# K first, weight words in one row, and the state's update joined to P U: a DeltaNet and SwiGLU kernel on one core

## The chip, the core and the metric

The kernel runs on one core of a Trainium2 chip. The core has a matrix engine (TensorE, PE in the profile, whose weight loads are shown apart as PEld), a vector engine (VectorE, DVE), an activation engine (ScalarE, ACT), a general engine (GpSimd, POOL) and an engine that only issues transfers (SyncE, SP). Each runs its own list of instructions in order, and waits at an instruction until the semaphores that it names have been counted up. The metric is the time of one execution on the device in microseconds (us); the median of several executions is given.

## The reference

The first stage is a delta rule with a state of 48 x 48 for each of 4 x 8 heads, over 768 steps. The second is a feed-forward layer on the 3072 rows of 384 that come out of it.

```python
k_n = k / (np.linalg.norm(k, axis=-1, keepdims=True) + 1e-06)
for t in range(S):
    y[:, :, t] = q_t @ state
    v_old = state @ k_t
    state = state + beta_t * outer(k_t, v_t - v_old)
# x = y, its heads side by side: (3072, 384)
xn = x / sqrt(mean(x * x) + 1e-06) * rms_g
out = (silu(xn @ w_gate) * (xn @ w_val)) @ w_out
```

The weights (384 x 1536 twice, and 1536 x 384) are 64-bit numbers: the kernel takes each apart into its 32-bit words and makes a 32-bit number of them. Everything is computed in 32-bit numbers.

## The kernel before

**Chunks.** The 768 steps are cut into 12 chunks of 64. For a chunk, `norms` makes the norms of K, `prep` the triangular system of the chunk and its inverse, `qpart` the matrix P of the products of Q and K, and `recur` uses them. `prep` transposes K (helper `turn`, L509), multiplies K by itself (`scores`, L532), writes the products to DRAM (dkk) and reads them back in another layout (at), scales them by beta (L646), and makes the inverse in 15 steps of a product and a sum on VectorE (L693, L699). The result (x or acc, L716, L720) goes through DRAM again (dx) into mt, m1bd and x2bd; two merges (L775, L799) fill its last block. `recur` multiplies the state by K and by Q (L840), forms r (L854), multiplies by the inverse to get u (`mr`, L886), and adds P U to the output (`pu`, L900). It normalises the rows (L940 to L990) and transposes them into xf (L986), and it adds K U to the state (`ku`, L1019, then L1028).

**Feed-forward.** Chunks 0 and 1 go through `ffn_plain`: L1064 multiplies by w_gate and w_val, L1071 takes Silu, L1072 forms hf, L1046 multiplies by w_out. From chunk 2 on, `ffn` forms two chunks' halves with 15 products in place of 18 (L1157, gathered by L1167 and L1169), and `down` multiplies by w_out with 7 in place of 8 (L1214). The factors for these are made once, by `factors` (L1122).

**Weights.** `weights` brings 18 pieces of 128 x 768 numbers into three buffers (`raw`), in SP's queue. For each, L460 on ScalarE scales the high words, L448 and L451 on VectorE shift and mask bits of it, L456 forms the other part from the low words, and the two are added: on TensorE, with a copy after it, for the first three pieces (L472, L473, L477), on VectorE for the rest (L480).

**Order.** The program is not issued in the order of the code. `Plan.add` records each operation with an engine, an assumed duration, a priority and the keys that it reads and writes. `Plan.run` builds an order in 60 rounds, each with slightly altered priorities (`SHAKE`, and the generator's seed), and keeps the one whose assumed end is earliest. A transfer's `after` is the time in this plan before which it isn't placed; on the chip it is no wait, and only the transfer's place in its queue comes of it. `op.port` makes the plan keep such operations of VectorE and GpSimd apart in time. PSUM's eight banks are handed out in the plan as groups come free. Until 70 us of the plan, gaps on TensorE are filled with multiplications of the identity by itself into a spare bank (`fillers`, L1312), which nobody reads.

Of the kernel before, what the change touches and what calls it, by code (L numbers as in the profile page):

```python
# [11 lines left out]
FP32 = mybir.dt.float32  # L12
U32 = mybir.dt.uint32
# [14 lines left out]
STICK = 1.0  # L28
SHAKE = 0.25

# [21 lines left out]
def fillers(a, b):  # L52

    n, t = 0, max(a, 2.0)
    while t < b - 0.3:
        n, t = n + 1, t + (0.43 if t < 6.5 else 0.26)
    return n


class Plan:  # L60
# [150 lines left out]
    def run(self, free, filler=None, until=0.0):  # L211
        self.first_priorities()
        best = None
        self.ends = []
        rng = random.Random(19)
        for k in range(ROUNDS):
# [30 lines left out]
def kernel(  # L247
# [96 lines left out]
    raw = [more[:, 1536 * i : 1536 * i + 1536].bitcast(I64) for i in range(NRAW)]  # L344
    cvb = [tflat[:, 512:1280], more[:, 4608:5376]]
    o_sb = [tmp[:, 3 + p, 0:DM] for p in range(2)]
    extra = [more[:, 3072 * h : 3072 * h + 3072].rearrange("p (x m n) -> p x m n", x=2, m=6) for h in range(2)]
    exkeys = [[("raw", 0), ("raw", 1)], [("raw", 2), ("o", 1)]]

# [70 lines left out]
    def weights():  # L420
# [14 lines left out]
        for n, (dst, src, keys) in enumerate(todo):  # L435
            pr = (30 if n < 9 else CV2) + 0.2 * n
            i, a = n % NRAW, n % NCV
            parts = dst.shape[1]
            rdst = raw[i].rearrange("p (a c) -> p a c", a=parts)
            dma(rdst, src, (0.1 if n == 0 else 3 + 2 * n), w=[("raw", i)], dur=0.7, work=3.06, after=(0.8, 5.0, 16.7, 24.5, 24.5, 33.3, 50.0)[n] if n < 7 else 53.0)  # L440
            words = raw[i].bitcast(U32).rearrange("p (a n two) -> p a n two", a=parts, two=2)
            low, high = words[:, :, :, 0], words[:, :, :, 1]
            u = dst.bitcast(U32)
            cc = cvb[a].rearrange("p (a n) -> p a n", a=parts)
            cvk = [("o", 1)] if a else [("tmp", 1), ("tmp", 2)]

            def s2(u=u):
                nc.vector.tensor_scalar(out=u, in0=u, scalar1=3, scalar2=None, op0=ALU.logical_shift_left)  # L448

            def s4(u=u, cc=cc):  # L450
                nc.vector.tensor_scalar(  # L451
                    out=cc.bitcast(U32), in0=u, scalar1=0xFF800000, scalar2=None, op0=ALU.bitwise_and
                )

            def s5(low=low, cc=cc, by=2.0**-52):
                nc.vector.scalar_tensor_tensor(out=cc, in0=low, scalar=by, in1=cc, op0=ALU.mult, op1=ALU.mult)  # L456

            P.add("ACT", 0.84, lambda high=high, dst=dst: nc.scalar.activation(out=dst, in_=high.bitcast(FP32), func=ACTF.Prelu, scale=2.0**-112, alpha=2.0**32), pr, r=[("raw", i)], w=[("cvw", n)])  # L460
            P.add("DVE", 0.66, s2, pr, w=[("cvw", n)])
            P.add("DVE", 0.66, s4, pr, r=[("cvw", n)], w=cvk)
            P.add("DVE", 1.0, s5, pr, r=[("raw", i)], w=cvk)
            done = []
            if n < NPE:
                for x_ in range(2):
                    ps = Group()
                    cut = slice(2 * x_, 2 + x_)
                    m = 512 - 256 * x_

                    def s6(ps=ps, dst=dst[:, cut], cc=cc[:, cut], m=m):
                        nc.tensor.matmul(ps.t[:, 0:m], ident, dst, start=True, stop=False)  # L472
                        nc.tensor.matmul(ps.t[:, 0:m], ident, cc, start=False, stop=True)  # L473

                    P.add("PE", 0.0035 * m, s6, pr, r=cvk + [("cvw", n), "ident"], w=[("cvp", n, x_)], ps=ps, size=8)
                    done.append(("cv", n, x_))
                    P.add("ACT", A(m), lambda dst=dst[:, cut], ps=ps, m=m: nc.scalar.copy(dst, ps.t[:, 0:m].rearrange("p (a n) -> p a n", n=256)), pr, r=[("cvp", n, x_), ("cvw", n)], w=[done[-1]], last=ps)  # L477
            else:
                done.append(("cv", n))
                P.add("DVE", 0.97, lambda dst=dst, cc=cc: nc.vector.tensor_tensor(out=dst, in0=dst, in1=cc, op=ALU.add), pr, r=cvk, w=[("cvw", n), done[-1]])  # L480
            for key in keys:
                ready.setdefault(key, []).extend(done)
# [4 lines left out]
    def load(c, what):  # L487
        t0 = c * C
        pk, pq, pv = ((-5, 1, 12), (5, 29, 36))[c] if c < 2 else (due(c, 150), due(c, 99), due(c, 70))
        for key, t, src, pr in (("k2", k2[c % NK], k, pk), ("q2", q2, q, pq)):  # L490
            for g in range(2):
# [3 lines left out]
                s = src.rearrange("b (y g) t e -> g t (b y) e", g=2)[g, t0 : t0 + C]  # L495
                dma(dst, s, pr, w=[(key, c % NK if key == "k2" else 0, g)], dur=0.7, work=1.02, eng="ACT" if c == 0 and g and key == "k2" else "SP", after=((0.8, 0.0, 0.0), (7.8, 20.8, 0.0))[c]["kqv".index(key[0])] if c < 2 else 60.3)
        if "v" in what:
            for bb in range(2):
                s = v[2 * bb : 2 * bb + 2, :, t0 : t0 + C, :].rearrange("p h t e -> t (p h) e")
                dma(vt[64 * bb : 64 * bb + 64], s, pv, w=[("v", bb)], dur=0.85, work=1.02, after=(30.4, 34.6)[c] if c < 2 else 60.0)  # L500

# [75 lines left out]
    def prep(c):  # L577
# [61 lines left out]
        for par in range(2):  # L639
            dma(at_[64 * par : 64 * par + 64].rearrange("p j t -> p (j t)"),  # L640
                dk.rearrange("i g x j t -> (i g x) (j t)"), pd, r=dkeys, w=[("at", par)], dur=0.56, work=1.8, eng="SP" if par or c else "ACT")
        bt = beta_b[:, c]
# [175 lines left out]
    def recur(c):  # L818
# [93 lines left out]
        for h in halves:  # L912
# [4 lines left out]
            for bb in range(2):  # L917
# [6 lines left out]
                else:  # L924
                    P.add("DVE", V(192 * len(h)), lambda dst=dst, f=src: nc.vector.tensor_copy(out=dst, in_=f()), pr, r=[gu[bb]], w=w, last=gu[bb])
        for h in halves:
            gy = groups(psy, h)
            P.rows = 64
            P.add("PE", 0.49 * len(h), lambda h=h: pu(h), py, r=ptk + uk(h), w=gy, ps=gy, size=64 * len(h))
            P.rows = 128  # L930
# [62 lines left out]
        if c > 1:  # L993
            X = lambda a, n, step=1: xf[:, a : a + step * (n - 1) + 1 : step]
            for dst, a, b_, op, n in (
# [10 lines left out]
                    out=dst, in0=a, in1=b_, op=op  # L1006
                ), pxv, r=[("xp", 0)], w=["xc", ("xp", 1)])
        if c < NCH - 1:
            pss = [Group(), Group()]

            def ku():
                for b in range(B):
                    for j in range(2):
                        for d in range(2):
                            for g in range(2):
                                rows = slice(64 * g, 64 * g + 64)
                                x_ = 4 * b + 2 * j + d
                                n = 48 * (2 * b + j)
                                nc.tensor.matmul(pss[g].t[64 * d : 64 * d + D, n : n + D], kn[rows, x_, 0:D], u_[rows, x_])  # L1019

            P.rows = 64
            P.add("PE", 0.98, ku, py + 2, r=kkeys_(c) + [("k2p", c % NK)] + uk((0, 1)), w=pss, ps=pss, size=128)
            P.rows = 128
# [237 lines left out]

    setup()
    load(0, "kqv")
    load_small()
# [81 lines left out]
```

## Time and profile before

| | |
|---|---|
| median of 3 executions | 717.38 us (717.36 to 718.38) |
| the profiled execution | 717.67 us |
| its span, first to last instruction | 716.0 us |
| TensorE busy | 701.5 us (98%) |
| VectorE busy | 553.6 us (77%) |
| ScalarE busy | 314.0 us (44%) |
| GpSimd busy | 152.7 us (21%) |
| transfers | 54.68 MB |
| mean granted clock of TensorE | 0.993 |

Times in the profile count from the start of the span. A busy TensorE is not one at its peak: the ends of matmuls are modelled, so that a short wait inside a run of them can be hidden in the busy time. The starts of weight loads (PEld) show it better. PEclk is the clock that TensorE was granted, in tenths of the full one, over 40 slices of 17.9 us. "<-" in square brackets names what ended an idle time. The queues SPq and ACTq show when transfers were issued, not when they landed.

### The profile page before, as it was taken

The numbers are of one execution on the slowest core, as the hardware profiler recorded it, in microseconds if no ns is written. First come the engines' busy times: TensorE is split into PE (matmuls) and PEld (weight loads), VectorE is DVE, ScalarE is ACT, GpSimd is POOL, SyncE is SP. The second block draws the span as 40 slices with busy tenths as digits, with TensorE's granted clock in tenths as the row PEclk, the third lists the DMA queues.
The fourth block names the chain that finished last, engine by engine and source line by source line (L and its number), as shares of the span: only waits on it lengthen the run. The fifth ranks groups of instructions, "written<-read, shape, count | busy, mean of one in ns | idle before, by whom it ended". The sixth has DMA issues, their size and how long they took to land.

```text
span 716.0 us, 23540 instructions
## 1 busy us (share of the span) xinstructions
PE 701.5 (98%) x10178; PEld 652.9 (91%) x10178; DVE 553.6 (77%) x1128; ACT 314.0 (44%) x732; POOL 152.7 (21%) x150
## 2 busy tenths in 40 slices
PE   8998999999999999999999999999999999999997
PEld 7797877777799999998999999999999999999997
DVE  4898999998967958947967967975968958847473
ACT  5613654232345436354345255355355354344331
POOL 4200307004315132204213303203213231000000
PEclk9997999999999999999999999999999999999999
DMA  8756798141154251242234153153162071030000
GB/s 171 210 124 165 157 261 219 23 66 43 35 90 77 39 111 28 47 72 60 57 59 83 37 96 61 34 88 64 38 109 47 12 118 27 15 63 2 23 1 23
DMA packets 210071, 54.68 MB, mean 76 GB/s; under 512 B 199216, under 2 KB 202288, under 8 KB 209968
## 3 DMA queue, kind: packets, MB, share of 16 engines
q1 hardware_dynamic: 205120, 52.26, 36.3%
q8 instruction: 80, 1.31, 0.8%
q10 hardware_dynamic: 4848, 0.92, 0.7%
q14 instruction: 23, 0.19, 0.1%
HBM read 40.83 MB, written 12.32 MB: 74 GB/s over the span
## 4 chain that ended last, share of the span: by engine, by line
PE 80%; DVE 15%; DMA 2%; issue 2%; SPq 1%; ACT 0%; DVEq 0%
PE bank L1157 38%; PE bank L1214 18%; PE bank L1064 6%; PE bank L1046 3%; PE bank L840 3%; PE bank L532 2%; DVE acc L699 2%; PE bank L509 2%; PE bank L799 2%; PE bank L886 2%; DVE acc L693 1%; DMA beta_b<-in_beta_dram 1%; PE bank L900 1%; DVE w_in L480 1%; PE bank L775 1%
## 5 line engine op out<-in xcount | busy, mean ns | idle before, releaser
L1167 DVE TENSOR_TENSOR tmp<-tmp,bank 128x512 f32<-128x512 f32 x180 | 122.0, 685 | 85.4 <-PE bank L1157 74.5
L1157 PE MATMUL bank<-xf,w_in 128*128 128x128 f32 x1440 | 181.5, 277 | 0.0
L1157 PEld LDWEIGHTS bank<-xf,w_in 128*128 128x128 f32 x1440 | 169.8, 192 | 2.3 <-issue 0.4
L1157 PE MATMUL bank<-xf,more 128*128 128x128 f32 x960 | 124.8, 277 | 0.0
L1157 PEld LDWEIGHTS bank<-xf,more 128*128 128x128 f32 x960 | 115.6, 192 | 1.7 <-DVE tmp L1167 0.4
L1169 ACT COPY tmp<-bank 128x512 f32<-128x512 f32 x120 | 68.6, 584 | 82.4 <-PE bank L1157 58.2
L699 DVE TENSOR_REDUCE acc<-acc 128x30 f32<-128x90 f32 (+4 forms) x180 | 85.1, 473 | 6.2
L1173 ACT ACTIVATE tmp<-tmp 128x256 f32<-128x256 f32 x120 | 49.7, 416 | 88.5 <-DVE tmp L1167 88.1
L693 DVE TENSOR_TENSOR acc<-acc,at 128x60 f32<-128x60 f32 (+4 forms) x180 | 63.5, 353 | 8.7 <-POOL at L676 5.9
L1214 PE MATMUL bank<-wo_sb,hf 128*128 128x192 f32 x360 | 63.8, 328 | 0.0
L1174 DVE TENSOR_TENSOR hf<-tmp 128x256 f32<-128x256 f32 x120 | 51.9, 445 | 12.9 <-ACT tmp L1173 11.6
L1214 PEld LDWEIGHTS bank<-wo_sb,hf 128*128 128x128 f32 x360 | 58.2, 190 | 0.3
L646 POOL TENSOR_TENSOR at<-at,beta_b 128x1024 f32<-128x1024 f32 x10 | 25.7, 2574 | 145.2 <-DMA at<-dkk 122.4
L1312 PE MATMUL bank<-ident 128*128 128x128 f32 x298 | 42.0, 304 | 1.4 <-POOL ident masks.py:199 1.4
L554 POOL TENSOR_TENSOR knrm<-ksum,half 128x16 f32<-128x16 f32 x12 | 35.9, 2992 | 33.8 <-DVE ksum L553 33.8
L720 POOL COPY acc<-acc 128x128 f32<-128x128 f32 x40 | 17.1, 458 | 116.4 <-DVE acc L699 115.6
L1312 PEld LDWEIGHTS bank<-ident 128*128 128x128 f32 x298 | 39.5, 215 | 2.5 <-POOL ident masks.py:199 1.4
L1046 PE MATMUL bank<-wo_sb,hf 128*128 128x384 f32 x96 | 34.3, 491 | 0.3 <-DVE r L854 0.3
L1064 PE MATMUL bank<-xf,w_in 128*128 128x256 f32 x144 | 33.6, 382 | 0.0
L1064 PE MATMUL bank<-xp,w_in 128*128 128x256 f32 x144 | 33.4, 383 | 0.0
L1064 PEld LDWEIGHTS bank<-xf,w_in 128*128 128x128 f32 x144 | 26.8, 190 | 4.9
L1064 PEld LDWEIGHTS bank<-xp,w_in 128*128 128x128 f32 x144 | 26.7, 190 | 4.4 <-issue 0.2
(164 smaller groups left out, 1045.9 us busy)
## 6 DMA issues: line engine op xcount, KB each, us to landing
at<-dkk SPq DMA_DIRECT2D x23, 256.0 KB, 3.9
q<-in_q_dram SPq DMA_DIRECT2D x24, 192.0 KB, 3.7
more<-in_moe_w_gate_dram SPq DMA_DIRECT2D x6, 768.0 KB, 6.1
more<-in_moe_w_val_dram SPq DMA_DIRECT2D x6, 768.0 KB, 6.3
more<-in_moe_w_out_dram SPq DMA_DIRECT2D x6, 768.0 KB, 7.5
vt<-in_v_dram SPq DMA_DIRECT2D x24, 192.0 KB, 4.1
out_dram<-tmp SPq DMA_DIRECT2D x48, 96.0 KB, 2.2
k<-in_k_dram SPq DMA_DIRECT2D x23, 192.0 KB, 3.8
```

Source lines behind the costliest of these rows:

```text
L554: P.add("POOL", 2.95, lambda: nc.gpsimd.tensor_tensor(out=knrm[i2], in0=ksum[i2], in1=half, op=ALU.pow), pn, r=[("ksum", i2), "half"], w=[ ...
L693: nc.vector.tensor_tensor(out=acc[:, 1:3, 0:n, j + 2 : W].rearrange("p a i t -> p i a t"), in0=acc[:, old, 0:n, j : j + 2, None].to_broadc ...
L699: nc.vector.tensor_reduce(out=acc[:, new, 0:n, j + 2 : W], in_=acc[:, lo : lo + 3, 0:n, j + 2 : W].rearrange("p a i t -> p i t a"), axis=A ...
L1046: nc.tensor.matmul(po[p].t[:, 0:DM], hf[:, spot(f), 128 * p : 128 * p + 128], wo_sb[:, spot(f)], start=(f == f0), stop=(f == f1 - 1), skip ...
L1064: nc.tensor.matmul(ps.t[:, TOK * side : TOK * side + TOK], w_in[:, side, h_, 3 * t + i_, n : n + 128], x_[:, 2 * t : 2 * t + 2].rearrange( ...
L1157: nc.tensor.matmul(g.t[:, 128 * z : 128 * z + 128], fac[:, side, 128 * f : 128 * f + 128], xf[:, xs], start=(begin and z == 0), stop=False ...
L1167: P.add("DVE", V(512), lambda t=t, g=g: nc.vector.tensor_tensor(out=t, in0=t, in1=g.t, op=ALU.add), -1, r=[g], w=[tk], last=g)
L1169: P.add("ACT", A(512), lambda t=t, g=g: nc.scalar.copy(t, g.t), -1, r=[g], w=[tk], last=g)
L1173: P.add("ACT", A(256), lambda t=t: nc.scalar.activation(out=t[:, 0:256], in_=t[:, 0:256], func=ACTF.Silu), -1, w=[tk])
L1174: P.add("DVE", V(256), lambda t=t, f0=f0, p=p: nc.vector.tensor_tensor(out=hf[:, spot(f0) : spot(f0) + 2, 128 * p : 128 * p + 128], in0=t[ ...
L1214: nc.tensor.matmul(g.t[:, 0:192], a_[:, f], b_[:, f], start=(begin and f == 0), stop=(f == 5), skip_group_check=True)
L1312: nc.tensor.matmul(warm[:, 0:128], ident, ident)
```

## The change

Line numbers below are those of the kernel before; those of the changed kernel lie 3 to 30 lines further on.

- The first transfer on SP is now half of K, where it was Q; Q follows. The other half of K is on ScalarE's queue in both.
- The fillers ahead of the first work are 13, whatever the plan says; elsewhere a filler counts 0.24 us, where it was 0.43 or 0.26.
- The scaled high words of a weight go to a row of 768 numbers that lie together (`cva`, two copies, one in unused columns of xf, one at the end of more), where they went to the weight's final place. L448 shifts them there, L451 masks them from there, and only the last addition writes to the final place.
- For chunks 2 to 10 `ku` is issued within the operation of `pu`, with four banks taken together. For chunks 0 and 1 it stays apart.
- The `after` of the early transfers of K, Q, V, at and the weights are changed.
- The operations of `setup` no longer count for `op.port`.
- Seed 77 where it was 19, `SHAKE` 0.12 where it was 0.25, and the assumed durations of L448, L451, L456 (0.57, 0.57, 0.96) and of `ku` (0.76).

```diff
-SHAKE = 0.25
+SHAKE = 0.12
...
-    n, t = 0, max(a, 2.0)
+    if a == 0.0:
+        return 13
+    n, t = 0, a
     while t < b - 0.3:
-        n, t = n + 1, t + (0.43 if t < 6.5 else 0.26)
+        n, t = n + 1, t + 0.24
...
-        rng = random.Random(19)
+        rng = random.Random(77)
...
+    cva = [xf[:, 6:12].rearrange("p a n -> p (a n)"), more[:, 5376:6144]]
...
-after=(0.8, 5.0, 16.7, 24.5, 24.5, 33.3, 50.0)[n] if n < 7 else 53.0)
+after=(7.5, 5.0, 19.2, 27.2, 18.7, 33.3, 47.0)[n] if n < 7 else 48.8)
...
-            u = dst.bitcast(U32)
+            top, cc = cva[a], cvb[a]
+            u = top.bitcast(U32)
...
-            P.add("ACT", 0.84, lambda high=high, dst=dst: nc.scalar.activation(out=dst, in_=high.bitcast(FP32), func=ACTF.Prelu, scale=2.0**-112, alpha=2.0**32), pr, r=[("raw", i)], w=[("cvw", n)])
+            P.add("ACT", 0.84, lambda high=high, top=top: nc.scalar.activation(out=top, in_=high.bitcast(FP32), func=ACTF.Prelu, scale=2.0**-112, alpha=2.0**32), pr, r=[("raw", i)], w=cak)
...
-                        nc.tensor.matmul(ps.t[:, 0:m], ident, dst, start=True, stop=False)
+                        nc.tensor.matmul(ps.t[:, 0:m], ident, top, start=True, stop=False)
...
-                P.add("DVE", 0.97, lambda dst=dst, cc=cc: nc.vector.tensor_tensor(out=dst, in0=dst, in1=cc, op=ALU.add), pr, r=cvk, w=[("cvw", n), done[-1]])
+                P.add("DVE", 0.97, lambda dst=dst, top=tiled(top), cc=tiled(cc): nc.vector.tensor_tensor(out=dst, in0=top, in1=cc, op=ALU.add), pr, r=cvk + cak, w=[done[-1]])
...
-after=((0.8, 0.0, 0.0), (7.8, 20.8, 0.0))[c]["kqv".index(key[0])] if c < 2 else 60.3)
+after=((0.0, 1.4, 0.0), (8.6, 25.0, 0.0))[c]["kqv".index(key[0])] if c < 2 else 56.8)
...
-after=(30.4, 34.6)[c] if c < 2 else 60.0)
+after=(30.4, 40.0)[c] if c < 2 else 60.0)
...
-eng="SP" if par or c else "ACT")
+eng="SP" if par or c else "ACT", after=41.2 if c == 1 else 0.0)
...
+            if 1 < c < NCH - 1:
+
+                def both_u(h=h):
+                    pu(h)
+                    ku()
+
+                P.add("PE", 1.74, both_u, py, r=ptk + uk(h) + kkeys_(c) + [("k2p", c % NK)], w=gy + pss, ps=gy + pss, size=256)
+                P.rows = 128
+                continue
...
     setup()
+    for op in P.ops:
+        op.port = False
     load(0, "kqv")
```

## The prediction

> **What bounds the kernel now.** I read the page first, then the chain of waits, then the timeline of the first 130 us, since most of the edits are there.
>
> ```profile
> PE 701.5 (98%) x10178; PEld 652.9 (91%) x10178; DVE 553.6 (77%) x1128; ACT 314.0 (44%) x732; POOL 152.7 (21%) x150
> ...
> PEclk9997999999999999999999999999999999999999
> ```
>
> TensorE is the bound, and its clock is full but for one dip near 55 us. In the chain, in order of time (start us, length, what):
>
> ```profile
> 333.98 1.09 PE bank L1157 x8
> 335.06 1.08 PE bank L900 x64
> ...
> 342.30 0.89 PE bank L1157 x8
> ...
> 379.23 2.01 PE bank L840 x128
> ```
>
> These pieces give prices. Eight 128-column passes are 0.89, or 0.111 each; the same eight cost 1.09 where a block of small matmuls follows, so entering such a block costs 0.20. One block is 1.08, two in a row 2.01 and not 2.16, so leaving costs 0.15. Reading the other pieces in the same way, a pass is 0.112 (L1157), 0.1625 (L1214), 0.216 (L1064), 0.3225 (L1046), 0.109 (transposes); a small block is 0.93 (L840, L886, L900, L532, L751), 0.71 (L1019), 0.85 (L799), 0.43 (L775). The order of the program from the first L1064 (75.04 us) on holds 2400, 840, 288, 96 and 226 passes, 97 small blocks (22 of L840, 20 of L532, 11 each of L886, L900, L775 and L799, 10 of L1019, one of L751) worth 81.7 us, and 76 entries with 76 exits: 268.8 + 136.5 + 62.2 + 31.0 + 24.6 + 81.7 + 76 x 0.35 = 631.4 us. The last load ends at 711.3, 636.3 after the first. So only 4.9 us of that stretch are stalls, of which 2.5 lie at 124 us:
>
> ```profile
> 117.38 3.01 DVE L480 TENSOR_TENSOR w_in<-w_in,tmp 128x768 f32<-128x768 f32 x1
> ...
> 126.35 0.66 PE L509 MATMUL bank<-ident,k 128*128 128x128 f32 x4 [1.67 <-DVE hf L1072]
> ```
>
> There VectorE, 97% busy from 72 to 120 us, is late with hf because a sum of 0.96 took 3.01 beside GpSimd's scaling of at. The time is thus: start of the stream + 631.4 + stalls + a tail of 4.7 (to 716.0). What sets the start is the first 75 us:
>
> ```profile
> 7.83 0.84 ACT L550 ACTIVATE r<-k 128x768 f32<-128x768 f32 x1 [3.92 <-DMA k<-in_k_dram]
> ...
> 18.37 0.84 SPq L363 DMA_DIRECT2D dkk<-pt  x2
> ...
> 20.84 0.49 SPq L363 DMA_DIRECT2D at<-dkk  x1
> ...
> 24.64 0.91 ACT L460 ACTIVATE w_in<-more 128x768 f32<-128x768 f32 x1 [0.93 <-DMA more<-in_moe_w_gate_dram]
> ...
> 28.18 1.22 DVE L646 TENSOR_TENSOR at<-at,bk 128x1024 f32<-128x1024 f32 x1
> ```
>
> K lands at 7.83 because its half on SP is issued third, at 2.57; dkk leaves SP at 18.37 though pt is ready at 16.15, behind beta loads; L646 starts at 28.18 because a weight that came at 24.6 is converted ahead of it on VectorE. Later:
>
> ```profile
> 53.97 1.31 PE L751 MATMUL bank<-ident,mt 32*32 32x32 f32 x64 [1.54 <-DMA mt<-dx]
> 55.21 2.08 PE L1312 MATMUL bank<-ident 128*128 128x128 f32 x8
> 59.05 1.08 PE L775 MATMUL bank<-m1bd,kk 128*32 128x64 f32 x32 [1.77 <-DVE m1bd L764]
> 60.06 1.23 PE L1312 MATMUL bank<-ident 128*128 128x128 f32 x4
> 61.22 1.92 PE L799 MATMUL bank<-x2bd,yn 128*32 128x128 f32 x16
> 63.07 2.24 PE L1312 MATMUL bank<-ident 128*128 128x128 f32 x10
> ```
>
> The array runs at half clock here: L751 takes 1.11 and L799 1.07 for chunk 1 at full clock. And L775 waits for VectorE's m1bd, which stands in its order behind 13.3 us of conversions and steps (44.8 to 58.07).
>
> [...]0.213 per filler pass to 13 us, 0.111 after. [...]L451 reads 3x256 and writes 768 for w_in, and 768 to 768 for wo_sb:
>
> ```profile
> L451 DVE TENSOR_SCALAR more<-w_in x6: 944/949/953, 19.6 to 142.5; 128x768 uint32<-128x768 uint32 x6
> L451 DVE TENSOR_SCALAR more<-wo_sb x3: 559/560/560, 76.7 to 146.4; 128x768 uint32<-128x768 uint32 x3
> ```
>
> [...]
>
> **The change part by part.** *K first.* With its half at 0.79, K lands near 5.0 (the ACT half took 3.7 from 0.79). The 13 fillers hold TensorE to 1.41 + 26 x 0.2125 = 6.9, so transposes start 0.9 earlier, not 2.8. Then L519 at 7.9, L551 8.6, GpSimd's power 9.8 to 12.75 (2.92), pt 13.25 to 14.55: 1.6 ahead of 16.15. On SP, dkk is now moved ahead of the last two beta loads, so it leaves at 14.6 and 15.1; at is issued near 17.5 (before: 20.84), behind a weight issued at 16.2. By 5.4 from issue, as before, that weight lands at 21.6. VectorE from 14.55: L621 0.95, one conversion 2.15, sums and bk 1.4 to 19.1, second norm (power 2.9) to 22.2, pt 1.3, the other conversion 2.15: L646 at 25.7, 2.5 ahead. If the weight comes 1.4 later: 1.1 ahead.
>
> *Words in one row.* L448 goes from 0.684 to 0.556, L451 from 0.95 to 0.56, in the 12 w_in weights: 12 x 0.52 = 6.2 us of VectorE; wo_sb nothing. On the chain to L764 it doesn't show, since one more conversion is put there: three of 2.14, two sums of 0.98, L646 to L676 3.4, four steps 2.9 = 14.6 against 13.3 before. L646's 2.5 lead becomes 1.2 to 1.5 at L764 (56.6 for 58.07). From 72 us on it is worth some 4 us less in front of hf, with the same stream behind: the 2.5 stall at 124 should go. The row is in two copies, so L460 on ScalarE now waits for the sum two weights back; behind it queue Silu (L1071) and so L1046. VectorE is ahead there, so I take 0, at most 2.
>
> *Fillers.* 149 become 169. 34 stand ahead of L751: at 0.2225 each 7.6 from about 45.9, L751 at 53.5; [...]VectorE's m1bd is the later or equal, at 57.4 to 58.7, and TensorE no longer idles before L751. At full clock L775, yn, L799, copies and 5 fillers take 3.4 for the 6.2 from 59.05 to 65.24: L886 at 61 to 62. VectorE then loses less at L815 and L925 (1.15 and 1.16 before): steps end near 69.5 for 72.5, L716 (now ahead of L990 on ScalarE) 0.8, six L990 1.75: first L1064 at 72.3 for 75.04. Bounds: 71 and 74.5.
>
> *P U with the state's update.* The pair saves an entry and an exit, 0.35, where the update stood alone. But seven of the nine updates already stood beside another small block, and elsewhere the new order takes blocks apart: counted over it, 76 entries again. Gain 0 in passes. It asks for four PSUM banks at once; price unknown, 0 to 0.9 (one product) each, I take 0.1. State is ready earlier, which nobody waits for.
>
> *New order, loads released anew, setup without port.* These move instructions only; SP's order of weights changes (gate of the third column block falls from 35.5 to about 44), but each conversion still lies ahead of its L1064 by 5 us or more on VectorE's new order. Chunk 2's steps now start when GpSimd has done L646 to L676 (5.9 undisturbed, near 113), with five steps ahead of the next hf: hf at 117.7 and 120.7, its L1046 at 120.3: stall 0.5. I put stalls at 1.0 to 195 us (before 3.0) and 2.0 after (before 1.9).
>
> Sum: 72.3 + 631.4 + 3.0 + 4.7 = 711.4 in place of 716.0. The profiled execution took 717.67, the median is 717.38, 1.4 over the span: 712.8.
>
> **Rivals.** *The start gain is eaten:* half clock persists after 44 us, fillers run late into L751, L886 comes at 64.5. [...]Start 74.5, stalls 4.9: 716.9. *Everything lands:* clock full throughout, start 70.8, stalls 1.5: 709.8. Against: fillers before L751 and L716's wait. *Slower, by banks:* the joint of P U and update waits for a product and its eviction at nine places, 0.9 each over the forecast: 720.9; it decides from 0.5 each (4.6/9). For it: seven or eight banks are in use; against: the one stall of 1.1 at 332 us is all that such scarcity costs now. *The change does nothing to the late stream* is part of the forecast: no passes or entries are saved.
>
> **Numbers.** Forecast 0.58 (711 to 715.9), everything lands 0.17, eaten 0.15, banks or another late stall 0.10. A tenth of "eaten" and none of banks is faster; faster 0.76, same 0.14, slower 0.10, with 0.2% (1.4 us) about what this kernel's measurement can tell. The range 709.0 to 717.2 leaves out some 0.08 above and 0.05 below.
>
> **What would show it.** First L1064 within 71 to 74.5; L646 on VectorE at 25.7; L451 at 0.56 throughout; PE clock full or dipping before 50 us, not at 55; no PE stall near 124; passes to the end 631 plus under 4. Wrong if L1064 starts after 74.5, or if new PE waits of 0.5 stand at the joined blocks.

## The result, and the profile after

| | before | after |
|---|---|---|
| median of 12 executions each, taken side by side | 718.21 us | 717.26 us |
| lowest and highest | 715.21, 719.11 | 715.40, 720.95 |
| ratio, 95% interval | | 0.9995 (0.9978 to 1.0012) |
| the profiled execution | 717.67 us | 717.62 us |
| its span | 716.0 us | 715.9 us |

No difference can be told. The forecast was 712.8 us with a range from 709.0 to 717.2; the median lies 4.5 us above the one and 0.06 above the other.

In the profile after, lines stand 3 to 30 further on: L1064 is now L1080, L1046 is L1062, L1071 and L1072 are L1087 and L1088, L886 is L891, L900 is L905, L646 to L676 are L651 to L681, L1122 is L1138. The page first: busy time by engine, and the granted clock in 40 slices of 17.9 us.

```profile
PE 702.8 (98%) x10218; PEld 653.9 (91%) x10218; DVE 548.9 (77%) x1128; ACT 313.2 (44%) x732; POOL 150.3 (21%) x150
...
PEclk9999999998999999999999999999999999999999
```

The dip near 55 us has gone (granted clock 1.00 from 53.5 to 60 us; it was 0.50 from 54.65 to 64.89), and VectorE has 4.7 us less to do. But there is a dip to 8 in the slice from 161 to 179 us that was not there before.

The start came as forecast. From the timeline (start us, length us, engine, line, what, and in brackets the idle time before and what ended it), the chain of chunk 0:

```profile
5.32 0.84 ACT L555 ACTIVATE r<-k 128x768 f32<-128x768 f32 x1
...
14.19 0.84 SPq L366 DMA_DIRECT2D dkk<-pt  x2
...
18.13 0.49 SPq L366 DMA_DIRECT2D at<-dkk  x1
...
21.40 0.93 ACT L464 ACTIVATE xf<-more 128x768 f32<-128x768 f32 x1 [0.62 <-DMA more<-in_moe_w_gate_dram]
...
25.17 1.22 DVE L651 TENSOR_TENSOR at<-at,bk 128x1024 f32<-128x1024 f32 x1
```

and that of chunk 1, to the first feed-forward product:

```profile
53.51 1.11 PE L756 MATMUL bank<-ident,mt 32*32 32x32 f32 x64
...
56.20 0.84 DVE L769 COPY m1bd<-bank 32x256 f32<-32x256 f32 x2
...
57.19 0.65 PE L780 MATMUL bank<-m1bd,kk 128*32 128x64 f32 x32 [1.04 <-DVE m1bd L769]
...
58.41 1.07 PE L804 MATMUL bank<-x2bd,yn 128*32 128x128 f32 x16
...
60.93 1.25 PE L891 MATMUL bank<-vt,mt 64*64 64x48 f32 x64
...
72.14 2.76 PE L1080 MATMUL bank<-xf,w_in 128*128 128x256 f32 x12
```

L756 takes 1.11 and not 1.31, L780 0.65 and not 1.08, at the granted clock of 1.00. The first weight load of L1080 is at 72.03 us, where it was at 75.04.

L455, the mask, by instruction (minimum, median and maximum in ns):

```profile
L455 DVE TENSOR_SCALAR more<-more x9: 554/560/1819, 15.5 to 149.3; 128x768 uint32<-128x768 uint32 x9
L455 DVE TENSOR_SCALAR tmp<-xf x9: 560/561/649, 23.7 to 139.2; 128x768 uint32<-128x768 uint32 x9
```

0.56 throughout, as forecast; 1.82 is one instruction, at 75.68 us, beside GpSimd's L626 (75.61 to 77.09).

So the stream of products started 3.0 us earlier, with the same passes, the same 76 entries, and the last load begins at 711.11 where it began at 711.18. The 3.0 us, and the 2.5 of the stall at 124 us, which is gone too, went between 149 and 171 us. The timeline there:

```profile
155.19 0.41 DVE L1088 TENSOR_TENSOR hf<-tmp,bank 128x256 f32<-128x256 f32 x1
...
157.16 0.38 ACT L1087 ACTIVATE tmp<-bank 128x256 f32<-128x256 f32 x1 [1.06 <-PE bank L1080]
...
158.04 2.46 PEld L1080 LDWEIGHTS bank<-xf,w_in 128*128 128x128 f32 x12 [0.20 <-issue]
...
158.38 2.56 POOL L651 TENSOR_TENSOR at<-at,beta_b 128x1024 f32<-128x1024 f32 x1 [26.18 <-DMA at<-dkk]
...
158.77 2.73 DVE L1138 TENSOR_TENSOR more<-more,w_in 128x512 f32<-128x512 f32 x1
...
161.02 2.03 POOL L676 TENSOR_TENSOR acc<-at 128x512 f32<-128x512 f32 x1
161.42 2.19 DVE L1138 TENSOR_TENSOR more<-w_in 128x512 f32<-128x512 f32 x1
...
163.53 0.74 DVE L1088 TENSOR_TENSOR hf<-tmp,bank 128x256 f32<-128x256 f32 x2
...
164.04 2.29 PE L891 MATMUL bank<-r,mt 64*64 64x48 f32 x64 [3.14 <-issue]
...
166.26 2.93 PE L1062 MATMUL bank<-wo_sb,hf 128*128 128x384 f32 x4
...
169.11 1.72 PE L905 MATMUL bank<-u,pt 64*64 64x48 f32 x64
```

L1138 forms the factors of the later chunks (24 sums, and L1136 has two more) that nobody needs before 201 us. Alone one takes 0.69. The two that meet GpSimd's L651 and L676, the scaling of at for chunk 3, take 2.73 and 2.19. They stand in VectorE's order ahead of two hf products, of which one could have run from 157.5 on (its Silu, L1087, ends there). hf comes at 163.5, the banks that it reads are free then, and L891 starts at 164.04. The bracket says "issue" and names no engine; that it is a bank waiting for hf is read from the times (the first of the two hf ends at 163.94), and the runs below try it. TensorE stopped for 3.14, and its granted clock was 0.50 from 163.58 to 170.41 in the trace: L891 takes 2.29 for 1.15, four passes of L1062 2.93 for 1.56.

Piece by piece against the prices of the prediction, the stretch has 1.55 (a wait for hf at 151 us) + 3.17 + 1.17 + 1.37 + 0.58 = 7.8 us more than its work. After 171 us there is 0.4 in one place and nothing else. The share of busy time from 160 to 180 us (us of the stretch, then busy us and instructions of PE, PEld, DVE, ACT, POOL, then the clock, the DMA share and GB/s) after,

```profile
160.00:180.00 20.00, 16.86 (x236) 12.86 (x235) 15.05 (x31) 4.77 (x12) 10.55 (x9) 0.83 0.12 22
```

and before:

```profile
160.00:180.00 20.00, 20.00 (x242) 15.19 (x241) 16.46 (x27) 5.55 (x12) 7.84 (x5) 1.00 0.20 46
```

### The profile page after: what moved, and what is told of

It is laid out like the page before. It is cut to its first block, busy times and chain, and to the rows that moved or that the text cites. A ratio compares the mean times of both kernels' runs of the same rounds, so it can differ in the third digit from the quotient of the medians.

```text
span 715.9 us, 23619 instructions
## 1 busy us (share of the span) xinstructions
PE 702.8 (98%) x10218; PEld 653.9 (91%) x10218; DVE 548.9 (77%) x1128; ACT 313.2 (44%) x732; POOL 150.3 (21%) x150
## 3 DMA queue, kind: packets, MB, share of 16 engines
q8 instruction: 80, 1.31, 0.8%
## 4 chain that ended last, share of the span: by engine, by line
PE 81%; DVE 11%; DMA 3%; POOL 2%; issue 2%; SPq 0%; ACT 0%; ACTq 0%; POOLq 0%; DVEq 0%
PE bank L1173 38%; PE bank L1230 19%; PE bank L1080 4%; PE bank L537 3%; PE bank L845 3%; DVE acc L704 2%; PE bank L514 2%; PE bank L1062 2%; DVE acc L698 2%; PE bank L905 2%; DMA more<-in_moe_w_val_dram 2%; PE bank L891 2%; PE bank L1330 2%; PE bank L804 1%; PE bank L942 1%
## 5 line engine op out<-in xcount | busy, mean ns | idle before, releaser
L1190 DVE TENSOR_TENSOR hf<-tmp 128x256 f32<-128x256 f32 x120 | 55.6, 476 | 9.0 <-ACT tmp L1189 8.1
L651 POOL TENSOR_TENSOR at<-at,beta_b 128x1024 f32<-128x1024 f32 x10 | 25.1, 2510 | 128.0 <-DMA at<-dkk 112.3
L725 POOL COPY acc<-acc 128x128 f32<-128x128 f32 x40 | 18.7, 496 | 129.3 <-DVE acc L704 128.8
L1330 PE MATMUL bank<-ident 128*128 128x128 f32 x338 | 44.0, 288 | 1.4 <-POOL ident masks.py:199 1.4
L1330 PEld LDWEIGHTS bank<-ident 128*128 128x128 f32 x338 | 41.6, 202 | 2.2 <-POOL ident masks.py:199 1.4
L1062 PE MATMUL bank<-wo_sb,hf 128*128 128x384 f32 x96 | 35.9, 510 | 1.1 <-DVE hf L1088 1.1
L1080 PE MATMUL bank<-xf,w_in 128*128 128x256 f32 x144 | 34.0, 383 | 0.0
L1080 PE MATMUL bank<-xp,w_in 128*128 128x256 f32 x144 | 32.9, 381 | 0.0
L1080 PEld LDWEIGHTS bank<-xp,w_in 128*128 128x128 f32 x144 | 27.0, 190 | 4.6
L1080 PEld LDWEIGHTS bank<-xf,w_in 128*128 128x128 f32 x144 | 26.6, 190 | 4.8 <-issue 0.2
```

The costliest lines, as they stand in the source:

```text
L1062: nc.tensor.matmul(po[p].t[:, 0:DM], hf[:, spot(f), 128 * p : 128 * p + 128], wo_sb[:, spot(f)], start=(f == f0), stop=(f == f1 - 1), skip ...
L1080: nc.tensor.matmul(ps.t[:, TOK * side : TOK * side + TOK], w_in[:, side, h_, 3 * t + i_, n : n + 128], x_[:, 2 * t : 2 * t + 2].rearrange( ...
L1190: P.add("DVE", V(256), lambda t=t, f0=f0, p=p: nc.vector.tensor_tensor(out=hf[:, spot(f0) : spot(f0) + 2, 128 * p : 128 * p + 128], in0=t[ ...
L1330: nc.tensor.matmul(warm[:, 0:128], ident, ident)
```

## The experiments

**How they are compared.** The prediction's sum holds for every kernel here: first load of L1064/L1080 + 604.7 of passes and blocks + 0.35 for each entry and exit + stalls = start of the last load, and 4.8 more is the span. With the counted entries that leaves the stalls, as what is over, from one profiled execution each:

| kernel | start | entries | stalls | last load | median | ratio to before, 95% interval |
|---|---|---|---|---|---|---|
| before | 75.04 | 76 | 4.8 | 711.18 | 718.21 | |
| after | 72.03 | 76 | 7.8 | 711.11 | 717.26 | 0.9995 (0.9978 to 1.0012) |
| hf_first | 71.36 | 76 | 3.9 | 706.58 | 712.50 | 0.9931 (0.9910 to 0.9952) |
| hf_first_all | 72.31 | 76 | 1.6 | 705.22 | 712.30 | 0.9930 (0.9905 to 0.9954) |
| at_later | 73.13 | 76 | 4.5 | 708.98 | 714.72 | 0.9956 (0.9939 to 0.9972) |
| before_hf_first | 74.37 | 76 | 6.9 | 712.56 | 718.26 | 1.0026 (1.0012 to 1.0040) |
| before_hf_both | 73.55 | 76 | 3.7 | 708.60 | 716.69 | 0.9994 (0.9982 to 1.0006) |
| before_k_first | 73.60 | 76 | 4.8 | 709.66 | 715.36 | 0.9982 (0.9966 to 0.9997) |
| before_row | 73.58 | 76 | 11.9 | 716.81 | 724.56 | 1.0098 (1.0063 to 1.0133) |
| after_norow | 72.87 | 76 | 9.2 | 713.40 | 719.62 | 1.0030 (1.0016 to 1.0044) |
| norow_hf_first_all | 72.91 | 76 | 3.2 | 707.43 | 715.29 | 0.9969 (0.9953 to 0.9985) |
| no_join | 73.19 | 83 | 3.0 | 709.93 | 716.79 | 0.9990 (0.9978 to 1.0003) |
| old_seed | 76.69 | 77 | 9.1 | 717.43 | 721.90 | 1.0063 (1.0045 to 1.0080) |

The first four kernels after "before" are the same program up to 133 us at least, and start at 71.4 to 73.1: a start from one trace is good to about 0.9 us. The interval of the medians decides where less is at stake. Kernels were run beside before in three groups, whose medians for before were 716.8, 717.1 and 716.9.

The edit that most of the runs use takes operations out of the finished plan and puts them behind another one; their numbers are those of `Plan.add`:

```diff
+MOVES = [((609, 610), 629)]
...
         self.end = best[0]
+        for ns, to in MOVES:
+            picked = [x for x in best[1] if x[0].n in ns]
+            rest = [x for x in best[1] if x[0].n not in ns]
+            i = [x[0].n for x in rest].index(to) + 1
+            best = best[0], rest[:i] + picked + rest[i:]
```

### Two sums out of the way of hf

The diff above on the changed kernel: 609 and 610 are the two stretched sums, 629 is the copy of u. (There are 26 factor sums, not the 48 of the expectation.)

> The changed kernel with two of VectorE's 48 factor sums (the two that took 2.73 and 2.19 us at 158.8 and 161.4) moved behind the two hf products and the copy of u that stood behind them; nothing else moves. Theory of the collision (two sums stretched by GpSimd's scaling of at make hf late, TensorE stops 3.1 us at 160.9 and its clock is halved for it): L891 starts near 161 in place of 164.0, no half clock, stalls from 149 to 171 us fall from 7.8 to 1.5 to 2.5, the time falls by 5 to 6 us to about 711.7, ratio to before 0.991 to 0.993. Theory of the joined product (four PSUM banks asked for at once hold up the stream): nothing gained, within 1 us of 717.3, ratio 0.9985 to 1.000. Theory of the clock (the half clock comes of itself near 164 us, and the stop is part of it): half clock stays, at most 1.3 us gained.

712.50 us, ratio 0.9931: against the changed kernel's 0.9995 that is 0.64%, or 4.6 us. The timeline (lines stand 6 further on than in the changed kernel: L657 is the scaling, L1144 the sum, L1094 hf, L897 chunk 2's L891):

```profile
156.68 3.45 DVE L1144 TENSOR_TENSOR w_in<-w_in,more 128x512 f32<-128x512 f32 x2
157.18 2.40 POOL L657 TENSOR_TENSOR at<-at,beta_b 128x1024 f32<-128x1024 f32 x1 [24.96 <-DMA at<-dkk]
...
160.05 2.22 DVE L1144 TENSOR_TENSOR more<-w_in 128x512 f32<-128x512 f32 x1
...
162.19 0.74 DVE L1094 TENSOR_TENSOR hf<-tmp,bank 128x256 f32<-128x256 f32 x2
...
162.70 1.48 PE L897 MATMUL bank<-r,mt 64*64 64x48 f32 x64 [1.84 <-issue]
```

The mechanism is cured in part: the scaling came 1.2 us earlier here and met two of the sums that were left. But the stop is 1.84 and not 3.14, and the granted clock is 1.00 from 155 to 172 us. The stall of 1.5 at 151 us stays, so that 3.3 us are left from 149 to 171 and not the 1.5 to 2.5 expected. Neither four banks at once nor a clock that falls of itself explains a gain of 4.6 us from moving two sums.

### All hf products ahead of the sums

```diff
-MOVES = [((609, 610), 629)]
+MOVES = [((142, 143, 144, 145), 529), ((605, 606, 599, 600, 601), 535), ((608, 609, 610), 629)]
```

> The same with every hf product from 146 to 163 us put ahead of the factor sums and of the one conversion that stood before it (three hf products move ahead; eight sums and four operations of a conversion come later). Theory of the collision and of a late VectorE: the stop of 1.1 us at 151 us goes too, stalls from 149 to 171 us are 0.5 to 1.5, time near 710.7, ratio 0.989 to 0.992. If the moved sums only make other work late (the steps of chunk 3, the first products L1173), the stall comes back at 165 to 205 us and the ratio is that of the first run or above. Joined product: ratio 0.9985 to 1.000.

In the trace, L897 starts at 160.98 without a wait, though GpSimd works from 158.60 on:

```profile
158.60 2.76 POOL L657 TENSOR_TENSOR at<-at,beta_b 128x1024 f32<-128x1024 f32 x1 [26.09 <-DMA at<-dkk]
...
159.06 0.41 DVE L1094 TENSOR_TENSOR hf<-tmp,bank 128x256 f32<-128x256 f32 x1
...
160.98 1.15 PE L897 MATMUL bank<-r,mt 64*64 64x48 f32 x64
```

No stall above 0.3 us lies between 149 and 171 us, and 1.6 us are all that is left of them in the whole stream. The span is 710.0; the median, 712.30, is 1.6 above what was expected and no better than the first run's within the intervals: the 2.3 us fewer stalls of the two traces do not show in the medians. Both kernels beat before and after.

### GpSimd out of the way of the sums

```diff
-        op = P.add(eng, dur, lambda: queue.dma_start(out=dst, in_=src), prio, r, w, lat=0.7)
+        op = P.add(eng, dur, lambda: (nc.scalar if op.n in ACTQ else queue).dma_start(out=dst, in_=src), prio, r, w, lat=0.7)
...
+MOVES = [((668, 669), 627)]
+ACTQ = (668, 669)
```

> The changed kernel with one thing moved: the two loads of at for chunk 3 leave later, from ScalarE's queue behind the yn copies at 159.8 us, and not from SP at 153.8. VectorE's order is untouched; GpSimd's scaling of that at now starts near 164.5 in place of 158.4, after the sums. Theory of the collision: the two sums take 0.69 each, hf is ready at 159.5 and 161.5, L891 starts at 161, no half clock there, stalls from 149 to 171 us fall from 7.8 to 1.5 to 3; chunk 3's steps L698 start 4 us later, which has some 20 us of room; time 711.5 to 714, ratio 0.992 to 0.996. If VectorE's order alone makes hf late (not GpSimd), the stop at 161 us stays and the ratio is 0.999 to 1.003.

The edit did something else in one part: the loads now stand behind the scaling in the program, so at of chunk 3 is loaded after it and is used without beta, and the scaling (on what was there before) ran at 133.4 us. What is left of GpSimd's work comes after the sums (lines 7 further on):

```profile
161.31 0.68 DVE L1145 TENSOR_TENSOR more<-w_in 128x512 f32<-128x512 f32 x1
162.03 0.69 DVE L1145 TENSOR_TENSOR more<-more,w_in 128x512 f32<-128x512 f32 x1
...
164.09 1.15 PE L898 MATMUL bank<-r,mt 64*64 64x48 f32 x64
...
166.73 1.78 POOL L683 TENSOR_TENSOR acc<-at 128x512 f32<-128x512 f32 x1 [30.99 <-ACT r L562]
```

With VectorE's order as in the changed kernel, every sum takes 0.69, L898 follows without a wait, and the mean granted clock of the execution is 1.000. From the hf ahead of the seven sums to the one behind them VectorE takes 4.80 us here (158.44 to 163.24) and 8.34 in the changed kernel (155.19 to 163.53): the stop at 161 us is of the meeting and not of VectorE's order alone. L898 is not at 161 as expected but at 164.1, since the start was 1.1 later here, the wait for hf near 152 us grew to 2.4, and at 133.4 us the scaling met another sum (L492, 3.14 for 0.95), which made an hf 0.8 us late. 714.72 us is 0.7 above what was expected; the ratio, 0.9956, is within it.

### The same cure for the kernel before

```diff
+MOVES = [((136, 137, 138, 139), 496)]
```

> The kernel before with the conversion of a wo_sb weight (four VectorE operations, 120.3 to 126 us) moved behind three hf products. Theory of the collision: the 2.5 us stall at 124 us goes, first L1064 stays at 75.0, time 2 to 2.5 us below before, ratio 0.9965 to 0.997. If the stall there is not of hf but of a bank or of the clock, the ratio is 1.000 within 0.001.

Not as expected: 718.26, ratio 1.0026. The stall at 124 us is gone, but there are 4.8 us at 166 to 173 us where there were none. The timeline of this kernel (6 lines further on than before):

```profile
163.47 2.36 POOL L652 TENSOR_TENSOR at<-at,beta_b 128x1024 f32<-128x1024 f32 x1 [20.38 <-DMA at<-dkk]
163.54 2.84 DVE L1128 TENSOR_TENSOR more<-w_in 128x512 f32<-128x512 f32 x1
...
166.31 2.88 DVE L1199 TENSOR_TENSOR wsum<-wo_sb 128x1152 f32<-128x1152 f32 x1
...
169.10 0.41 DVE L1078 TENSOR_TENSOR hf<-tmp,bank 128x256 f32<-128x256 f32 x1
...
169.56 2.70 PE L1052 MATMUL bank<-wo_sb,hf 128*128 128x384 f32 x4 [3.12 <-DVE hf L1078]
```

In the kernel before, chunk 3's scaling came at 166.62, behind the hf that counts:

```profile
166.11 0.41 DVE L1072 TENSOR_TENSOR hf<-tmp,bank 128x256 f32<-128x256 f32 x1
...
166.62 3.38 POOL L646 TENSOR_TENSOR at<-at,beta_b 128x1024 f32<-128x1024 f32 x1 [22.84 <-DMA at<-dkk]
```

With TensorE no longer held up at 124 us, and a start 0.7 earlier in this execution, it came at 163.47, ahead of it. This is what happened to the changed kernel, made by another edit: work that comes earlier moves the meeting to another place, and gives the gain back there.

Hf was then put ahead at both places:

```diff
-MOVES = [((136, 137, 138, 139), 496)]
+MOVES = [((136, 137, 138, 139), 496), ((610, 611, 612), 545), ((613, 618, 619, 620), 558)]
```

> The kernel before with hf put ahead at both places where a sum meets GpSimd's scaling: the conversion at 120 us as in the earlier run, and eight sums between 161 and 171 us behind the hf products there. Theory of the collision: neither the 2.5 us at 124 us nor the 4.8 us that came in its place at 166 to 173 us is there; stalls 1.5 to 2.5, start 75, so 75 + 631.3 + 2 + 4.8 + 1.4 = 714.5, ratio 0.9965. The gain of the whole change on equal footing is then the difference to 712.4: 2 us. If removing a stall here always brings one elsewhere (VectorE's load is the cause), stalls stay at 5 or more and the ratio at 0.999 or above.

Both stalls are gone from the trace, and 3.7 us in pieces of 1.2 at most are left, more than the 1.5 to 2.5 expected. The profiled execution took 715.10, near the expected 714.5, but by luck: its start, 73.55 for 75, makes up for the stalls. The median of 22 is 716.69, and the ratio, 0.9994, is the one that the expectation gave to its rival, that a stall removed here brings one elsewhere. What the other executions lose is not to be seen in one trace, and stays open: in the kernel before, putting hf ahead gained nothing that can be told. By ratios, the change is worth 0.6% once hf is ahead in both kernels (0.9930 against 0.9994), with the same reservation.

### K first alone

The order of before is kept; Q's two loads go behind K's, the last beta load and g behind dkk, and 13 fillers lead.

```diff
+    if a == 0.0:
+        return 13
     n, t = 0, max(a, 2.0)
...
+MOVES = [((17, 16), 14), ((23, 28), 172)]
```

> The kernel before, its order kept, with three moves at the start alone: K's half leads SP's queue, dkk stands ahead of the last beta load and g, 13 fillers at first in place of 10. The prediction's steps: K transposes at 6.9 (7.85 before), pt ready near 14.6 (16.15), at issued near 17.5 (20.8), L646 at 25.7 to 27, first L1064 at 73.5 to 74, time 1.0 to 1.5 us lower, ratio 0.998 to 0.9986. Rival, that the start's gain of 3.0 us is of the new order alone: m1bd and L1064 stay where they were (58.1 and 75.0), ratio 1.000.

At 1.3 us (0.9982) as expected: K transposes at 6.2, dkk at 13.6, at issued at 17.5, L646's answer at 26.79, m1bd at 56.70, first product at 73.60. Half clock persists here (L775's answer takes 1.08 for 0.65): so the full clock near 55 us comes of another part of the change. It is full there too in the runs below that take the row, the joint or the order out of the changed kernel (mean granted clock 0.998 in after_norow, whose half clock is after 164 us, and 1.000 in no_join; L780 takes 0.65 in old_seed). Among what is left are the fillers' new count and the loads; neither was tried alone.

The stalls after the start are as long as before, but not the same. None is at 124 us. In its place TensorE stops at 112.5 us, with one half clock of 3.41 us behind it:

```profile
111.42 1.09 PE L848 MATMUL bank<-state,qt 48*64 48x48 f32 x63
...
114.63 0.34 PE L848 MATMUL bank<-state,qt 48*64 48x48 f32 x1 [2.12 <-issue]
```

The stop lies inside one operation, ahead of the last of its 64 multiplications, and no record there has a wait. In the thirteen traces ten stops of the weight loads over 0.75 us, after 20 us, have no wait in them. Each ends 1.26 to 1.66 us after the end of a transfer of 16 KB in the queue of the kind "instruction" (here 112.07 to 113.24). Most of these transfers, 80 in a run, pass without such a stop. What TensorE waits for there is not shown by the traces, and no run tries it. The stop of 3.14 us in the changed kernel is of another kind: its first weight load has a wait, and the last such transfer ahead of it ended at 158.48.

### The one row alone, and the change without it

Both use an order written out in full, that of the kernel that they are made from, so that little but the row differs. In `before_row` the row's two copies force seven of ScalarE's L460 to come later than in before; each is put at the first place at which its copy is free in the order.

```diff
-            P.add("DVE", 0.66, s2, pr, w=[("cvw", n)])
-            P.add("DVE", 0.66, s4, pr, r=[("cvw", n)], w=cvk)
...
+            P.add("DVE", 0.57, s2, pr, w=cak)
+            P.add("DVE", 0.57, s4, pr, r=cak, w=cvk)
```

> The kernel before with the words in one row and nothing else, in the order of before; seven of ScalarE's conversions L460 have to come later in it, as the row is in two copies. Theory of the collision (what stops TensorE is a sum beside GpSimd's scaling, not VectorE's load): L451 falls from 0.95 to 0.56 in the twelve w_in weights, 6.2 us of VectorE, and the time falls by at most 1.5 us, by an earlier m1bd alone; a stall of 1 to 3 us stays between 116 and 128 us; ratio 0.998 to 1.000. Theory of the load (the prediction's: 6.2 us less on VectorE end the 2.5 us stall): no stall there, first L1064 near 74, ratio 0.9945 to 0.997. If ScalarE's later conversions hold up Silu: slower, up to 1.003.

724.56 us, 7 us slower than before, where at most 1.003 was thought possible. The timeline (8 or 9 lines further on than before; L468 is ScalarE's conversion, L489 is the sum, L530 the copy of qt, L518 a transpose):

```profile
119.95 0.99 PE L518 MATMUL bank<-ident,q 128*128 128x128 f32 x4 [3.38 <-issue]
...
122.03 2.37 DVE L489 TENSOR_TENSOR w_in<-xf,tmp 128x768 f32<-128x768 f32 x1
...
124.42 0.91 ACT L468 ACTIVATE xf<-more 128x768 f32<-128x768 f32 x1 [7.23 <-DVE w_in L489]
125.23 0.57 ACT L530 COPY qt<-bank 128x512 f32<-128x512 f32 x1
```

ScalarE stands 7.23 us at a conversion that waits for the sum two weights back, and 3.72 and 3.53 us at two earlier ones; behind each are qt's or kt's copy and Silu, which have banks to free. This is the side risk that the prediction took at 0 (at most 2). But it does not account for the 7 us. The two shorter waits lead to stops of TensorE at 85.8 and 91.3 us, 1.25 and 1.36 us between weight loads. The long one leads to none: TensorE works from 119.95 to 126 us. Its largest stop, 3.38 us with a half clock of 3.41 us behind it, ends 4.5 us before ScalarE moves; it is one of the ten without a wait, beside an instruction transfer from 117.24 to 118.29. With its half clock it is some 5 of the 11.9 us of stalls. How much of the 7 us is the row's stays open. Part of ScalarE's wait is again the meeting: L459, L464 and L489 ahead of it took 1.71, 2.98 and 2.37 beside GpSimd, for 0.56, 0.96 and 0.95.

The other way round, the words back in their final place in the changed kernel's own order:

```diff
-            P.add("DVE", 0.57, s2, pr, w=cak)
-            P.add("DVE", 0.57, s4, pr, r=cak, w=cvk)
...
+            P.add("DVE", 0.66, s2, pr, w=[("cvw", n)])
+            P.add("DVE", 0.66, s4, pr, r=[("cvw", n)], w=cvk)
```

> The changed kernel in its own order with the words back in their final place, as before. VectorE has 6.2 us more, of which 1.5 to 2 us ahead of m1bd. Theory of the collision: first L1080 at 73.3 to 74 for 72.0, the sums at 158 us come later still beside GpSimd and the stalls from 149 to 171 us grow from 7.8 to 9 or 11; time 719 to 721, ratio 1.002 to 1.005. Theory that the row's gain is hidden: within 0.5 us of the changed kernel, ratio 0.999.

719.62, 2.4 us above the changed kernel, inside the expectation; stalls 9.2 for 7.8, start 72.87 for 72.03. And the same with hf ahead:

```diff
+MOVES = [((142, 143, 144, 145), 529), ((605, 606, 599, 600, 601), 535), ((608, 609, 610), 629)]
```

> The changed kernel with the words in their final place again and with the hf products ahead as in the run that had stalls of 1.6. It tells what the one row is worth where no hf stands behind a sum. Theory of the collision: the 6.2 us of VectorE are hidden but for the start (72.9 for 72.0 to 72.3) and a late conversion or two: stalls 2 to 4, time 713 to 715, 1 to 2.5 over the same kernel with the row. Theory of the load: as without the moves, stalls of 6 or more, time 717 to 719.

715.29, 3.0 above the same kernel with the row; start 72.91, stalls 3.2, of them 2.0 in front of chunk 2's L891 again, where two sums that were left ahead of hf took 3.56 beside GpSimd. So in the order of the change the row is worth 2.4 to 3.0 us, with these moves or without.

### The joined product

```diff
-            if 1 < c < NCH - 1:
+            if False:
                 def both_u(h=h):
...
-            if c < 2:
+            if c < NCH:
                 P.rows = 64
```

> The changed kernel with P U and the state's update as two products again, as before; the order is planned anew from it, so it moves instructions everywhere. Theory of the joined product (four banks at once cost time): faster than the changed kernel by 2 to 5 us, with fewer stalls after 200 us. Theory of the collision: the passes, 76 entries and the start (72 to 73) stay, and the time is 631.4 + start + tail + the stalls that this order happens to have where GpSimd's scaling of at meets VectorE's sums (110 to 175 us): between 711 and 719; after 200 us at most 2.5 us of stalls, as in the kernels before and after.

716.79 us, in the expected band and not below the changed kernel by more than the intervals allow (0.9990 against 0.9995). The 76 entries do not stay as expected: the new order has 83, so 7 x 0.35 = 2.5 us more of TensorE's time. It has fewer stalls, the largest, 2.9 us, at 163 us, where two sums beside GpSimd took 5.00 together and L1062 waited 2.81 for hf. After 200 us it loses 1.0, and the changed kernel, with a joint in each of nine chunks, 0.4: no stop shows that the joint would hold up. The order is another one too, so this run does not price the joint alone.

### Another order

```diff
-SHAKE = 0.12
+SHAKE = 0.25
...
-        rng = random.Random(77)
+        rng = random.Random(19)
```

> The changed kernel with the number that its random search starts from and the size of its shake as before (19 and 0.25 for 77 and 0.12): every edit but these is kept, and another order comes out. Theory of the collision: start at 71 to 73.5, stalls from 100 to 175 us anywhere from 1 to 9 us by which VectorE operation meets GpSimd's scaling, time 710 to 719, and each stall over 1 us has a VectorE operation of two SBUF inputs stretched to twice its length in front of a late hf, m1bd or r. Theory that the edits themselves (joined product, one row, K first) cost the stalls: stalls of 6 us or more at the same place, chunk 2's L891, and the time within 1 us of 717.3.

721.90, 2.9 above the band, with a start of 76.69 that was not expected either: L905 of the first chunks stopped for 2.38 us in its middle, at 65.4 us, and a half clock of 3.41 us followed at 69.04, together about 4.1 us. This is another of the ten stops without a wait, beside an instruction transfer from 65.17 to 66.43. The stop of 3.26 us and the half clock behind it are at chunk 2's L891 as in the changed kernel, with the same signature: L1138 takes 2.73 and 2.21 beside L651 and L676 at 157.1 to 162.0, ahead of hf at 163.95. This run does not tell the two theories apart as it was meant to, since the place is the same; the runs with hf ahead do.

## Why the prediction was wrong

**Right, point by point.** K transposes were forecast at 6.9 and came at 6.75; at issued near 17.5, came at 17.7 and 18.1; the weight landing at 21.6, came by 21.4; L646's answer at 25.7, came at 25.17; m1bd at 57.4 to 58.7, came a little earlier, at 56.20 to 57.04; L886's answer at 61 to 62, came at 60.93; first product at 72.3, came at 72.03. Clock full before 50 us (granted 1.00 from 10 to 50 us), no stall at 124 us, GpSimd done for chunk 2 "near 113" (113.04), hf at 117.7 and 120.7 (118.17 and 120.61), 76 entries: all there. The passes from 72.03 on are the same count and the same sum, 631.3 (the small blocks add up to 81.6, where the prediction wrote 81.7), and the tail is 4.8, forecast 4.7. That the start agrees to 0.3 is in part luck: it moves by more than a microsecond from one execution to another (71.36 to 73.13 in the four kernels that start alike). So is the number of the rival "the start gain is eaten", 716.9: its late start, half clock and late fillers are not there.

**The step that failed** is "I put stalls at 1.0 to 195 us (before 3.0) and 2.0 after". They were 7.4 to 195 us and 0.4 after. 72.03 + 631.3 + 7.8 + 4.8 = 715.9, the span. It failed as a reading and not only as a size: the step worked out the one meeting of GpSimd with VectorE that the kernel before had suffered from, chunk 2's (to be over near 113 us), and found it cured; chunk 3's, near 158 us, was not worked out. The trace of before held the warning: sums of 0.69 nearly without a gap from 149 to 166 us, and GpSimd's scaling at 166.62, which was to come earlier with everything else. The new order and the durations put seven sums and two hf products into the very 5 us in which at lands.

The plan shows why nothing in the code stood in the way. Its own start times, beside those of the trace:

```
                                         plan     chip
hf ahead of the seven sums             149.93   155.19
last of the seven sums ends            154.63   163.61
GpSimd's scaling of at starts          154.63   158.38
chunk 2's L891 starts                  157.50   164.04
```

The plan lets one such operation start in the very hundredth of a microsecond in which the other ends, and leaves nothing between them. On the chip VectorE was 5.3 us behind the plan and the load of at only 3.75: enough to overlap.

The sum that started at 158.77, 0.39 after GpSimd's L651 (158.38), ended 0.56 after it (160.94 to 161.50); the next one started at 161.42, 0.40 after L676 (161.02), and ended 0.56 after it (163.05 to 163.61). The prediction saw such a sum at 117 us (3.01 for 0.96) and counted with it there alone. The two sums, of 0.69 each alone, cost 3.5 us together.

What brings a half clock after a stop is shown only in part. The half clock lasts 10.24 us in before (54.65 to 64.89), 6.83 in the changed kernel (163.58 to 170.41), and 3.41 behind each of six stops in other kernels. After 64 us, seven stops of the matmul records of 2.12 to 3.38 us had a half clock that began within 1.8 us of their end. One of 2.81 had none, nor any of 1.97 or less. So the length alone does not decide, and what else does stays open. The changed kernel drew 6.83 us of half clock where the other six stops drew 3.41: 3.1 of its 7.8 us.

**The row** was credited with the end of the stall at 124 us and nothing at the start. In sum that is near what it is worth (2.4 to 3.0), but 124 us is not where it comes from: after_norow has no stall there, and before_k_first and before_hf_first have none without the row either. Which of the earlier start and the new order ended it in the changed kernel was not told apart. "I take 0, at most 2" for ScalarE behind the row was right for the new order; in the old one the stops that can be laid to it are 2.6 us together.

**The joined product** at "gain 0 in passes" was right against before; the order planned without it has seven entries more, but another seed alone moves the count too (77 in old_seed). Its four banks cost nothing that shows. The stop of 1.1 us at 332 us in the kernel before, which the prediction read as a shortage of banks, is one of the ten without a wait, inside L840. **Chances:** "banks or another late stall" had 0.10, priced at 720.9 for the banks; the late stall had no price of its own. With the meeting at chunk 3 worked out by the same numbers (two sums held for 2 us each, hf 3.5 late, a stop of 3 us, possibly doubled) it would have been a rival of 716 to 719 with a chance of its own.

## What to carry to other kernels

Where an edit starts a stream earlier, every meeting of two engines whose instructions grow longer side by side moves with it (here GpSimd's scaling for chunk 3 from 166.62 to 158.38 us, and a sum of 0.69 took 2.73); work out all of them in the stretch behind it, and not only the one that hurt before. Fill work that nobody waits for was better placed here behind the operation that frees a bank than ahead of it, where it took 2.73 and 2.19 us for 0.69 beside another engine: moving two sums out of 26 behind hf made a change that measured as nothing into one of 0.7%. It is no sure gain: in the kernel before the same cure measured as nothing. A plan that keeps two engines apart without a margin keeps them apart only in the plan.

## What was not expected of the hardware

- The start of identical instructions moved between 71.4 and 73.1 us from one execution to another, and medians of the kernel before agreed to about 0.2%: a gain under 1 us is not read from one trace.
- Operations of VectorE with one source took longer beside GpSimd too: the mask of 768 words 1.71 in before_row and 1.82 in the changed kernel, for 0.56.
- What a stop of TensorE costs is not its length alone: 1.84 us cost 1.9, 2.81 cost 2.9, and 3.14 cost 6.3 (3.2, and 3.1 of half clock behind it), but 2.12 in before_k_first drew a half clock too.
- TensorE stopped ten times in these traces where no wait is on record, each time 1.26 to 1.66 us after the end of a 16 KB transfer of instructions. Read the brackets: "issue" ahead of a block was a bank in the changed kernel, and inside an operation it was nothing that the trace names.
